# Routing of the first block moved into the last dense turn's up products, and weight splits of the routed layer all on VectorE, in a retention + dense MoE + routed MoE kernel

## The chip, the cores and the metric

One core of one Trainium2 chip runs the whole kernel. The metric is the device time of one execution in microseconds; of several runs the median counts. TensorE (PE in the rows) multiplies, VectorE (DVE) and ScalarE (ACT) do elementwise work, GpSimd (POOL) does elementwise work too and issues indirect DMAs, and SyncE (SP) issues the plain DMAs. Every engine works through its own queue in program order and waits on semaphores of the others.

## The reference, cut to what matters

```
x = attention(q, k, v, lam)                      # N=1536 tokens, model width 512
# dense layer: all E=8 experts on all tokens, F=1024 hidden units, Sinkhorn-like weights P
out = sum_e P[:, e] * (relu(x @ w1[e]) @ w2[e])
# routed layer: every token goes to the one expert with its largest logit
logits = out @ w_gate2
expert_idx = argmax(logits, axis=1)
gate_w = softmax(logits)[arange(N), expert_idx]
final[mask_e] = gate_w * (relu(out[mask_e] @ v1[e]) @ v2[e])
```

Everything is float32. The kernel splits each float32 factor into two float32r parts, `hi` (a rounded copy, made by ScalarE) and `lo` (the rest, made by a subtraction), and takes three products of parts instead of one.

## The kernel before

The dense layer runs in sixteen sub-turns `s` (half an expert's hidden units each), and each of them in two turns `c` of six token tiles. A turn has two calls of `dense_up` (line 536; seven products of six matmuls of 128x384 each, with additions on VectorE between them) and then six tiles of down products (`dense_down`, line 579: twelve matmuls of 128x512 a tile, in two halves of six). `dense_add` (line 588) adds a tile to its sum `acc` on VectorE. `dense_up` calls `between()` at three places; in the last sub-turn that function takes one step from the list `late`.

When `acc` of a tile is complete, `gate2_a` (line 606) writes it to DRAM, transposes it on TensorE (`x2p`, line 611) and copies it by ScalarE; `gate2_b` takes the gate's logits from it (`l2p`, line 618). The routing then runs on VectorE in short instructions: `route_a` (from line 715; the expert of each token and running counts), `route_b` (TensorE, tiles `prank` and `count`), `route_c` (place in the block; `slot` is a 0/1 matrix of token by slot, written for each token tile), `route_first` and `route_first_b` (token numbers of block 0, tile `gid`), and at the end `route_blocks`, `route_slots` (`pid`), `route_experts` and `slot_gates`, `slot_gates_a`, `slot_gates_b` (weights of the slots; an exponential by series, `pgt`).

The routed layer works on blocks of 128 tokens of one expert. For block `b`: an indirect DMA gathers the tokens (`xg`, issued by GpSimd), TensorE transposes them (`xp`), `copy_x` splits them (`xb`), `up` multiplies (`hb`, 24 matmuls in two parts), `turn_h` transposes and splits the hidden units (`hp`, `ht`), `down` multiplies (`yb`, 24 matmuls), and an indirect DMA scatters the result. The weights of an expert are eight pieces of 512 KB; `splitv` (line 654) makes `hi` on ScalarE (line 664) and `lo` by a subtraction of 128x1024 (line 665) on the engine that it is given. `reload` fetches the next expert's pieces into the same room, as soon as the split pieces have been read, and only if the block has another expert.

What sets the order: the schedule is manual, so each engine's queue has the order in which the code issues its instructions. From line 1085 to line 1217 the code is written out by hand: the last six down tiles (called by `dd`), the routing, and the first three blocks, each step in its place. From block 2 on `segment` (line 1214) repeats a fixed order for every block. In the written-out part `splitv` and `split_next` are told which engine subtracts; in `segment` it is VectorE.

Of the kernel before, what the change touches and what calls it, by code (L numbers as in the profile page):

```python
# [10 lines left out]
F32 = mybir.dt.float32  # L11
# [8 lines left out]
P = 128  # L20
# [3 lines left out]
MAGIC = 12583039.0  # 1.5 * 2^23 + 127  # L24
# [7 lines left out]
def tile_retention_moe_moe(  # L32
# [50 lines left out]
    lower = const.tile([P, P], F32, name="lower")  # lower[p, m] = 1 where p < m  # L83
# [17 lines left out]
    # the dense layer takes the tokens in two thirds of CPC tiles of each batch  # L101
# [32 lines left out]
    def load_w2(s):  # L134
        e, o = divmod(s, 2)
        src = w2[e, o * FS:(o + 1) * FS, :].rearrange("(r p) d -> p r d", p=P)
        if s == 0:
            # where the output will be summed
            t = [hpool.tile([P, DM], F32, tag=f"acc{i}", name=f"raw2_0_{i}") for i in (5, 11, 7, 8)]
            for r in range(FS // P):  # L140
                nc.sync.dma_start(out=t[r], in_=src[:, r, :])
            raw[2, s] = t
            return
# [56 lines left out]
    # It leaves the factors of the dense layer: blocks of x^T and their sums, by the halves of  # L200
    # the model width and by the two batches.
# [26 lines left out]
    # decays: dmask[j, h2, pair, i] = lam^(i-j) for i >= j, qpow[(h2 d), pair, i] = lam^(i+1)  # L228
# [32 lines left out]
    def a_transpose(t):  # L261
# [12 lines left out]
        if c < CPB - 1:  # L274
            # from here on, the keys weigh in the state
# [122 lines left out]
    def exp_head(x, tmp):  # L398
        """exp(x) for x <= 0: 2^n by its bits, the rest by its series."""
# [136 lines left out]
    def dense_up(s, c, j, between):  # L536
        """Hidden units j*P.. of either half of FS, for the c-th third of tokens of each batch."""
# [49 lines left out]
    def dense_add(s, t, ps):  # L587
# [3 lines left out]
        if s == 0:  # L591
            # the gate is not ready yet
# [37 lines left out]
    def keep(name, shape, dtype=F32):  # L630
        """One tile for all blocks that take turns in it."""
# [4 lines left out]
    def load_first():  # L636
        # the factors of the dense layer make room, the first blocks before the others
# [16 lines left out]
    def splitv(which, b, j, engine=nc.vector):  # L654
# [14 lines left out]
    # Tiles of tokens in the order of the dense layer's turns; the rank of a token within its  # L669
    # expert is known before the tokens of later turns are.  # L670
# [12 lines left out]
    def route_start():  # L683
        # the blocks' hidden units will take the place of all but the last ones
# [15 lines left out]
        for space, sizes in (  # L700
# [4 lines left out]
            for name, a, b in sizes:  # L705
                r_[name] = space[:, :a * b].bitcast(F32R).rearrange("p (a b) -> p a b", b=b)
                space = space[:, a * b:]

# [568 lines left out]
```

## Time and profile before

| | |
|---|---|
| runs, us | 1337.42, 1331.64, 1329.52 (median 1331.64) |
| the profiled execution's own span | 1330.2 us |
| TensorE busy | 1294.4 us (97%) |
| VectorE busy | 882.5 us (66%) |
| ScalarE busy | 470.8 us (35%) |
| GpSimd busy | 215.2 us (16%) |
| mean granted TensorE clock | 0.986 |

The profile is one execution. In a timeline row stand the start and the duration (us from the span's start), engine, line, operation, output and inputs, their shape, and in brackets how long the engine had been idle and what ended that. PEclk is the granted TensorE clock as a share of 2.4 GHz; it has two levels, 2.4 and 1.2 GHz, so a mean of 0.5 in a stretch means half speed all through it.

### The profile page before, as it was taken

The page shows a single profiled execution, that of the slowest core. Times are in us where ns is not written, and L with a number is a line of the kernel's source. Part 1 is how long each engine was busy: PE and PEld are TensorE (multiplying, and loading weights), DVE is VectorE, ACT ScalarE, POOL GpSimd, SP SyncE. Part 2 cuts the span into 40 slices and gives each one's busy share as a digit, 9 for nine tenths or more (in the row PEclk, how much of TensorE's full clock was granted, in tenths as well). Part 3 has the DMA queues.
Part 4 walks back from the last instruction along what each step waited for, and adds up shares of the span by engine and source line. Part 5 has one row for each costly group of instructions (what it writes and reads, how often), then busy time and mean ns, then how long its engine had stood idle before and what let it go on. Part 6 is the DMA issues. An engine that isn't in the chain of part 4 may idle for free. (4 is left out here: it accounts for less than half of the span.)

```text
span 1330.2 us, 17688 instructions
## 1 busy us (share of the span) xinstructions
PE 1294.4 (97%) x6796; PEld 1144.2 (86%) x6796; DVE 882.5 (66%) x1464; ACT 470.8 (35%) x744; POOL 215.2 (16%) x179
## 2 busy tenths in 40 slices
PE   8999999999999999999999999999999998699998
PEld 6768899999999999999999999999999987578886
DVE  5757756665756656666666575665666466899886
ACT  3433433132222222222313222222222233588885
POOL 5740010101101010101010110101010024631221
PEclk9989999999999999999999999999999988799999
DMA  9610111010101110101001020210000401457463
GB/s 175 152 56 1 32 33 32 33 64 0 64 1 63 32 33 32 32 33 32 32 33 63 1 64 1 64 32 33 32 32 33 174 25 38 153 201 272 158 218 112
DMA packets 73353, 88.79 MB, mean 67 GB/s; under 512 B 41135, under 2 KB 41135, under 8 KB 73264
## 3 DMA queue, kind: packets, MB, share of 16 engines
q1 hardware_dynamic: 70624, 79.74, 19.3%
q0 software_dynamic: 2640, 7.87, 1.8%
q8 instruction: 55, 0.90, 0.3%
q14 instruction: 34, 0.28, 0.1%
HBM read 116.95 MB, written 7.08 MB: 93 GB/s over the span
## 5 line engine op out<-in xcount | busy, mean ns | idle before, releaser
L582 PE MATMUL y<-w2h,h 128*128 128x512 f32 x1536 | 486.6, 393 | 0.0
L529 PE MATMUL p<-xops,w1h 128*128 128x384 f32 x1792 | 455.9, 335 | 0.0
L582 PEld LDWEIGHTS y<-w2h,h 128*128 128x128 f32 x1536 | 290.0, 189 | 59.3
L529 PEld LDWEIGHTS p<-xops,w1h 128*128 128x128 f32 x1792 | 323.9, 188 | 2.4
L582 PE MATMUL y<-w2l,h 128*128 128x512 f32 x768 | 301.0, 392 | 0.0
L529 PE MATMUL p<-xops,w1l 128*128 128x384 f32 x896 | 299.9, 335 | 0.0
L595 DVE SCALAR_TENSOR_TENSOR acc<-y,pm,acc 128x512 f32<-128x512 f32 x180 | 134.9, 750 | 244.1 <-PE y L582 243.5
L545 DVE TENSOR_TENSOR u<-u,p 128x384 f32<-128x384 f32 x320 | 171.0, 551 | 47.6 <-PE p L529 44.0
L549 ACT ACTIVATE h<-u 128x384 fp32r<-128x384 f32 x192 | 101.0, 526 | 282.7 <-DVE u L545 282.7
L557 ACT COPY p<-p 128x384 f32<-128x384 f32 x64 | 30.6, 478 | 396.1 <-PE p L529 396.1
L582 PEld LDWEIGHTS y<-w2l,h 128*128 128x128 f32 x768 | 145.0, 189 | 28.9
L529 PEld LDWEIGHTS p<-xops,w1l 128*128 128x128 f32 x896 | 168.2, 188 | 0.0
L154 POOL TENSOR_TENSOR sums<-raw 128x512 f32<-128x512 f32 x16 | 21.4, 1336 | 814.0 <-DMA raw<-in_moe_w_dram 477.0
L550 DVE SCALAR_TENSOR_TENSOR h<-u,h 128x384 fp32r<-128x384 f32 x192 | 117.0, 609 | 14.2 <-ACT h L549 2.8
L665 DVE TENSOR_TENSOR vl<-room,vh 128x1024 fp32r<-128x1024 f32 x82 | 101.2, 1281 | 13.6 <-ACT vh L664 13.0
L664 ACT CAST vh<-room 128x1024 fp32r<-128x1024 f32 x88 | 88.2, 1061 | 10.5 <-DMA room<-in_moe_w_dram 10.5
L1064 PE MATMUL yb<-vh,ht 128*128 128x512 f32 x224 | 72.8, 396 | 0.0
L545 DVE TENSOR_TENSOR u<-p,p 128x384 f32<-128x384 f32 x64 | 35.3, 552 | 54.5 <-PE p L529 54.4
L1064 PE MATMUL yb<-vl,ht 128*128 128x512 f32 x112 | 44.6, 398 | 8.6 <-DVE vl L665 8.6
L1064 PEld LDWEIGHTS yb<-vh,ht 128*128 128x128 f32 x224 | 42.6, 191 | 9.7 <-DVE ht L1054 0.7
L1032 PE MATMUL hb<-room,xb 128*128 128x512 f32 x168 | 41.0, 394 | 0.0
L182 DVE TENSOR_TENSOR w2l<-raw,w2h 128x512 fp32r<-128x512 f32 x64 | 40.0, 686 | 1.2 <-ACT w2h L181 1.2
(220 smaller groups left out, 1227.2 us busy)
## 6 DMA issues: line engine op xcount, KB each, us to landing
room<-in_moe_w_dram SPq DMA_DIRECT2D x132, 512.0 KB
raw<-in_moe_w_dram SPq DMA_DIRECT2D x31, 1024.0 KB
q<-in_q_dram SPq DMA_DIRECT2D x12, 256.0 KB
k<-in_k_dram SPq DMA_DIRECT2D x12, 256.0 KB
v<-in_v_dram SPq DMA_DIRECT2D x12, 256.0 KB
x2d<-acc SPq DMA_DIRECT2D x12, 256.0 KB
raw<-in_moe_w_dram SPq DMA_DIRECT2D x4, 256.0 KB
xg<-x2d,gid POOLq DMA_INDIRECT x16, 4.6
```

Source lines behind the costliest of these rows:

```text
L182: nc.vector.tensor_tensor(out=lo, in0=raw[2, s][r], in1=f32(hi), op=ALU.subtract)
L529: nc.tensor.matmul(ps, lhsT=w[:, a, k, j * P:(j + 1) * P], rhs=xops[c][:, b, part, k, :], start=(n == 0), stop=(n == 5),)
L545: nc.vector.tensor_tensor(out=out, in0=in0, in1=in1, op=ALU.add)
L549: nc.scalar.activation(hi, x, AF.Relu)
L550: nc.vector.scalar_tensor_tensor(out=lo, in0=x, scalar=0.0, in1=f32(hi), op0=ALU.max, op1=ALU.subtract)
L557: nc.scalar.copy(p1, mul(A11, B11))
L582: nc.tensor.matmul(ps, lhsT=h[f][:, part, o * P:(o + 1) * P], rhs=w[:, f, :], start=(j == 0 and f == j and i == 0), stop=(j == 1 and f != ...
L595: nc.vector.scalar_tensor_tensor(out=acc[t], in0=ps, scalar=pm[:, t, e:e + 1], in1=acc[t], op0=ALU.mult, op1=ALU.add,)
L664: nc.scalar.copy(hi, t)
L665: engine.tensor_tensor(out=lo, in0=t, in1=f32(hi), op=ALU.subtract)
L1032: nc.tensor.matmul(ps, lhsT=x[:, kk, :], rhs=w[:, cols], start=(n == 0), stop=(n == 3 * KD - 1))
L1064: nc.tensor.matmul(ps, lhsT=h[:, f, :], rhs=w[:, f % 2, :], start=(n == 0), stop=(n == 3 * KF - 1),)
```

## The change

1. `splitv` and `split_next` have no engine to choose any more: every `lo` of the routed layer's weights is subtracted by VectorE. The six `slot` matrices of the first turn, too, are written by VectorE and no longer by GpSimd (`route_c` loses its engine).
2. The routing of the first block (`route_ones`, `route_a`, `route_b`, `route_c`, `route_first`, `route_first_b`, `gather(0)`) becomes four entries at the end of `late`, and so runs during the two `dense_up` calls of the last turn. It writes its six slot matrices to a place of its own (`early["slot"]`, in the former weights' room), since the final place still holds factors of the dense layer; they are written a second time, to the final place, after the second split.
3. The steps of the written-out part are reordered: transposes and logits of finished tiles come two tiles later or closer together, `route_slots` comes before `route_experts`, `up(1, 0)` comes ahead of the splits of block 1's second weights, and `slot_gates` with `slot_gates_a` moves from before and between those splits to after block 1's `turn_h`. The subtraction that `slot_gates` began with moves into `route_experts`.

```
-    def splitv(which, b, j, engine=nc.vector):
+    def splitv(which, b, j):
...
         nc.scalar.copy(hi, t)
-        engine.tensor_tensor(out=lo, in0=t, in1=f32(hi), op=ALU.subtract)
+        nc.vector.tensor_tensor(out=lo, in0=t, in1=f32(hi), op=ALU.subtract)
...
+        early["slot"] = words("raw", [P, KD, FS], F32R, "early_slot").rearrange(
+            "p (a b) -> p a b", b=P)
...
-    def route_c(p0, p1, engine=vt):
+    def route_c(p0, p1):
...
+        if p0 > 0:
+            slots(p0, p1, r_["slot"])
+
+    def slots(p0, p1, dst):
         for p in range(p0, p1):
-            engine.tensor_scalar(
-                out=r_["slot"][:, p], in0=ioff, scalar1=off[:, p - p0:p - p0 + 1], scalar2=None,
+            vt.tensor_scalar(
+                out=dst[:, p], in0=ioff, scalar1=r_["off"][:, p:p + 1], scalar2=None,
                 op0=ALU.is_equal,
             )
...
                     if o == 2 * CPC - 1:
                         late.append(gate2)
+                        late.append(lambda: (route_ones(), route_a(0, 2 * CPC)))
+                        late.append(lambda: route_b(0, 2 * CPC))
+                        late.append(lambda: (
+                            route_c(0, 2 * CPC), slots(0, 2 * CPC, early["slot"]), route_first()))
+                        late.append(lambda: (route_first_b(), gather(0)))
...
-    def split_next(which, b, j0, j1, engines=(nc.vector,)):
+    def split_next(which, b, j0, j1):
...
     ps = {}
-    route_ones()
-    route_a(0, n0)
-    splitv(1, 0, 0, nc.gpsimd)
-    splitv(1, 0, 1, nc.gpsimd)
+    g_a, g_b = (lambda i: gate2_a(turns[n0 + i])), (lambda i: gate2_b(turns[n0 + i]))
     dd(0, 0)
     dd(1, 0)
     dd(0, 1)
+    splitv(1, 0, 0)
     dd(1, 1)
+    splitv(1, 0, 1)
+    slots(0, n0, r_["slot"])
+    dd(2, 0)
+    g_a(0)
     splitv(1, 0, 2)
-    gate2_a(turns[n0])
-    route_b(0, n0)
-    route_c(0, n0, nc.gpsimd)
-    route_first()
-    dd(2, 0)
...
     run(ups)
     route_blocks()
     turn_h(0, (0,))
+    splitv(2, 0, 3)
+    route_slots()
     route_experts()
     reload(1, 1)
     reload(2, 1)
-    route_slots()
     turn_h(0, (1,))
     gather(1)
-    slot_gates()
     downs = down(0)
-    run(downs, 3 * KF - 4)
+    run(downs, 3 * KF - 6)
     turn_x(1, copies=False)
-    run(downs, 4)
+    run(downs, 6)
...
-    split_next(1, 1, 0, KD - 1, (v_, p_, v_))
+    split_next(1, 1, 0, KD - 1)
     copy_x(1)
     split_next(1, 1, KD - 1, KD)
-    slot_gates_a()
-    split_next(2, 1, 0, KD, (v_, p_, p_, p_))  # E1
     run(up(1, 0))
+    split_next(2, 1, 0, KD)
     run(up(1, 1))
     turn_h(1, (0,))
     turn_x(2)
     gather(4)
     turn_h(1, (1,))
-    split_next(1, 2, 0, KD, (v_, p_))  # E2
+    slot_gates()
+    slot_gates_a()
+    split_next(1, 2, 0, KD)
     downs1 = down(1)
     run(downs1, 2 * KF)
     slot_gates_b()
     run(downs1, KF)
-    split_next(2, 2, 0, KD, (v_, p_))  # E3
+    split_next(2, 2, 0, KD)
```

TensorE's queue in the last turn's second `dense_up`: `p_15_1_1` are its products (the number at the end tells them apart), first before, then of the change.

```order
L529 MATMUL p_15_1_1_8736<-xops_100,w1h_8253 128x384 x2
L529 MATMUL p_15_1_1_8736<-xops_100,w1l_8254 128x384
L529 MATMUL p_15_1_1_8744<-xops_100,w1h_8253 128x384 x2
L529 MATMUL p_15_1_1_8744<-xops_100,w1l_8254 128x384
L529 MATMUL p_15_1_1_8744<-xops_100,w1h_8253 128x384 x2
```

```order
L529 MATMUL p_15_1_1_8751<-xops_100,w1h_8253 128x384 x2
L529 MATMUL p_15_1_1_8751<-xops_100,w1l_8254 128x384
L750 MATMUL prank_8759<-early_x 128x48
L751 MATMUL prank_8759<-early_x 128x48
L529 MATMUL p_15_1_1_8762<-xops_100,w1h_8253 128x384 x2
```

The two `prank` products stand between the second and the third of the seven products now; the one `full` product comes after the fourth, and the six `pid` products after the seventh.

VectorE's queue from block 1's input split to the second weights of block 2: `vl` are weight parts, `xb` and `ht` the parts of inputs and hidden units, L874 to L885 before (L885 to L902 now) the slot gates. Before:

```order
L1019 TENSOR_TENSOR xb_1_9239<-xp_9193,xb_1_9238 128x512
L665 TENSOR_TENSOR vl_3_1_9243<-room_8478,vh_3_1_9242 128x1024
L874 TENSOR_TENSOR room_8479<-room_8478,tok_88 128x12x20
L416 SCALAR_TENSOR_TENSOR room_8478<-room_8478 128x96 x6
...
L884 CAST room_8479<-room_8478 128x12x20
L885 TENSOR_TENSOR room_8479<-room_8478,room_8479 128x12x20
L665 TENSOR_TENSOR vl_0_1_9284<-room_8478,vh_0_1_9283 128x1024
L1054 TENSOR_TENSOR ht_9216<-hp_0_9327,ht_9215 128x512
L1019 TENSOR_TENSOR xb_0_9340<-xp_9334,xb_0_9339 128x512
L1054 TENSOR_TENSOR ht_9216<-hp_1_9344,ht_9215 128x512
L665 TENSOR_TENSOR room_8479<-room_8478,room_8479 128x1024 x2
```

and now:

```order
L1035 TENSOR_TENSOR xb_1_9240<-xp_9192,xb_1_9239 128x512
L665 TENSOR_TENSOR vl_3_1_9244<-room_8478,vh_3_1_9243 128x1024
L665 TENSOR_TENSOR vl_0_1_9284<-room_8478,vh_0_1_9283 128x1024
L665 TENSOR_TENSOR vl_1_1_9288<-room_8478,vh_1_1_9287 128x1024
L665 TENSOR_TENSOR vl_2_1_9220<-room_8478,vh_2_1_9219 128x1024
L665 TENSOR_TENSOR vl_3_1_9222<-room_8478,vh_3_1_9221 128x1024
L1070 TENSOR_TENSOR ht_9217<-hp_0_9313,ht_9216 128x512
L1035 TENSOR_TENSOR xb_0_9326<-xp_9320,xb_0_9325 128x512
L1070 TENSOR_TENSOR ht_9217<-hp_1_9330,ht_9216 128x512
L885 TENSOR_SCALAR lg<-lg 128x96
...
L902 TENSOR_TENSOR room_8479<-room_8478,room_8479 128x12x20
L665 TENSOR_TENSOR room_8479<-room_8478,room_8479 128x1024 x4
```

The gates moved behind the hidden units of block 1, and VectorE has all four subtractions of each set.

GpSimd's queue from the start of the routed layer's work to the first scatter (`L1002` and `L819` are gathers). Before:

```order
L665 TENSOR_TENSOR room_8479<-room_8478,room_8479 128x1024 x2
L766 TENSOR_SCALAR room_8479<-ioff,room_8478 128x128 x6
L1002 DMA early_x<-x2d,gid 128x512
L665 TENSOR_TENSOR room_8479<-room_8478,room_8479 128x1024
L665 TENSOR_TENSOR early_l<-room_8478,early_h 128x1024 x3
L665 TENSOR_TENSOR early_r<-room_8478,early_r 128x1024
...
L665 TENSOR_TENSOR vl_1_1_9231<-room_8478,vh_1_1_9230 128x1024
L665 TENSOR_TENSOR vl_1_1_9288<-room_8478,vh_1_1_9287 128x1024
```

and now:

```order
L716 TENSOR_SCALAR early_x<-ones 128x8
L819 DMA early_x<-x2d,gid 128x512 x2
L819 DMA xg_9223<-x2d,gid 128x512
L819 DMA xg_9225<-x2d,gid 128x512
L819 DMA xg_9223<-x2d,gid 128x512
L1088 DMA out_dram<-room_8478,sid 1536x512
```

Fifteen subtractions and six slot matrices have left it; gathers and scatters remain.

## Rows read from the trace of the kernel before

**Rows 1.** Windows: busy time of PE, PEld, DVE, ACT, POOL; PEclk, DMA share, GB/s

```profile
1172.20:1320.00 147.80, 147.80 (x730) 123.94 (x729) 133.84 (x135) 129.07 (x169) 30.53 (x25) 1.00 0.60 211
```

**Rows 2.** Timeline of TensorE: its longest waits before 1172 us

```profile
1087.27 0.66 PE L611 MATMUL x2p<-ident,acc 128*128 128x128 f32 x4 [3.19 <-DVE acc L595]
1135.91 1.04 PE L1032 MATMUL hb<-vh,xb 128*128 128x512 f32 x2 [1.88 <-DVE xb L1019]
1153.08 0.79 PE L1064 MATMUL yb<-vl,ht 128*128 128x512 f32 x1 [8.59 <-DVE vl L665]
```

**Rows 3.** Windows as in rows 1: the stretch after the first of these waits

```profile
1088.00:1094.70 6.70, 6.70 (x23) 5.49 (x23) 2.73 (x11) 0.59 (x1) 3.50 (x6) 0.53 0.21 78
```

**Rows 4.** Timeline of VectorE: long instructions of the routing, slot gates and splits

```profile
1081.20 2.06 DVE L726 TENSOR_TENSOR early_x<-room,ioff 128x48 fp32r<-128x48 f32 x1
1083.37 3.18 DVE L730 TENSOR_TENSOR early_x<-early_x 128x8 fp32r<-128x8 f32 x6
1139.41 6.01 DVE L416 SCALAR_TENSOR_TENSOR room<-room 128x96 f32<-128x96 f32 x6
1147.07 2.36 DVE L884 CAST room<-room 128x240 fp32r<-128x240 f32 x1
1160.41 5.77 DVE L665 TENSOR_TENSOR vl<-room,vh 128x1024 fp32r<-128x1024 f32 x2
```

**Rows 5.** Single lines on VectorE: ns min/median/max, first and last start

```profile
L724 DVE TENSOR_TENSOR early_x<-early_x,ioff x3: 207/2264/2305, 1080.7 to 1117.6; 128x24 fp32r<-128x24 f32 x2, 128x48 fp32r<-128x48 f32 x1
L416 DVE SCALAR_TENSOR_TENSOR etmp<-etmp x6: 258/258/259, 114.8 to 116.3; 128x96 f32<-128x96 f32 x6
L874 DVE TENSOR_TENSOR room<-room,tok x1: 2574/2574/2574, 1136.9 to 1136.9; 128x240 fp32r<-128x240 f32 x1
L885 DVE TENSOR_TENSOR room<-room,room x1: 2426/2426/2426, 1149.5 to 1149.5; 128x240 fp32r<-128x240 f32 x1
L665 DVE TENSOR_TENSOR room<-room,room x27: 1209/1218/1221, 1087.8 to 1303.5; 128x1024 fp32r<-128x1024 f32 x27
```

**Rows 6.** Timeline of VectorE: the same kinds while GpSimd did nothing

```profile
1107.25 0.57 DVE L730 TENSOR_TENSOR early_x<-early_x 128x8 fp32r<-128x8 f32 x3
1124.87 0.41 DVE L834 TENSOR_TENSOR room<-room,row 128x240 fp32r<-128x240 f32 x1
```

**Rows 7.** Timeline of GpSimd: its first two subtractions

```profile
1080.77 4.75 POOL L665 TENSOR_TENSOR room<-room,room 128x1024 fp32r<-128x1024 f32 x2 [60.46 <-ACT room L664]
```

**Rows 8.** Timeline: end of VectorE's first `dense_up`; TensorE's last product, down products, third tile

```profile
1071.82 1.23 DVE L550 SCALAR_TENSOR_TENSOR h<-u,h 128x384 fp32r<-128x384 f32 x2
...
1077.39 0.51 PE L529 MATMUL p<-xops,w1h 128*128 128x384 f32 x2
1078.43 0.39 PE L582 MATMUL y<-w2h,h 128*128 128x512 f32 x1
1083.69 0.39 PE L582 MATMUL y<-w2h,h 128*128 128x512 f32 x1
1088.02 0.48 PE L582 MATMUL y<-w2h,h 128*128 128x512 f32 x1
```

**Rows 9.** Timeline of TensorE: one tile's distance; of VectorE: from `count` to `val`

```profile
1098.24 0.48 PE L582 MATMUL y<-w2h,h 128*128 128x512 f32 x1
1102.34 0.49 PE L582 MATMUL y<-w2h,h 128*128 128x512 f32 x1
1121.10 0.26 DVE L813 TENSOR_TENSOR room<-count,i 128x96 f32<-128x96 f32 x1 [0.36 <-PE count L743]
```

**Rows 10.** Timeline: `pid`, expert list, block 1's casts, its first activation, two kinds of splits

```profile
1125.33 1.77 PE L843 MATMUL pid<-room 128*128 128x20 f32 x12
1127.53 0.16 DVE L860 TENSOR_TENSOR other<-room 1x19 int32<-1x19 f32 x1
1129.50 2.95 ACT L664 CAST vh<-room 128x1024 fp32r<-128x1024 f32 x3 [1.26 <-DMA room<-in_moe_w_dram]
1140.14 0.60 ACT L1037 ACTIVATE room<-hb 128x512 f32<-128x512 f32 x1 [2.18 <-POOL vl L665]
1152.94 0.68 DVE L1054 TENSOR_TENSOR ht<-hp,ht 128x512 fp32r<-128x512 f32 x1
1169.22 4.63 DVE L665 TENSOR_TENSOR vl<-room,vh 128x1024 fp32r<-128x1024 f32 x4 [0.16 <-ACT vh L664]
```

More of the change, by code (lines that the diff above doesn't have):

```diff
@@ L707, in route_start @@
                 space = space[:, a * b:]
+        early["slot"] = words("raw", [P, KD, FS], F32R, "early_slot").rearrange(
+            "p (a b) -> p a b", b=P)
+        early["xg"] = [early["x"][:, b * DM:(b + 1) * DM] for b in range(2)]
     def route_ones():
@@ L800, in route_first_b @@
             nc.tensor.matmul(
-                pid[:, :2], lhsT=r_["slot"][:, p], rhs=r_["val0"][:, p],
+                pid[:, :2], lhsT=early["slot"][:, p], rhs=r_["val0"][:, p],
                 start=(p == 0), stop=(p == 2 * CPC - 1),
@@ L805, in route_first_b, with gather @@
             out=gid[:, 0:1], in0=pid[:, 0:1], scalar1=-1.0, scalar2=0.0, op0=ALU.add, op1=ALU.max
+        )
+    xg = {}
+    def gather(b):
+        xg[b] = early["xg"][b] if b < 2 else keep(f"xg{b % 2}", [P, DM])
+        nc.gpsimd.indirect_dma_start(
+            out=xg[b], out_offset=None, in_=x2d[:2 * CPC * P, :] if b == 0 else x2d,
+            in_offset=bass.IndirectOffsetOnAxis(ap=gid[:, b:b + 1], axis=0),
         )
@@ L861, in route_experts @@
         vt.tensor_copy(nal, end[0:1, E - 1:E])
-    def slot_gates():
         vt.tensor_tensor(
@@ L867, in slot_gates @@
         )
+    def slot_gates():
         vt.tensor_scalar_max(lgf, lgf, -87.0)
@@ L981, in tile_retention_moe_moe @@
     ereg = {}
-    xg, xt, xb, hb, ht = {}, {}, {}, {}, {}
+    xt, xb, hb, ht = {}, {}, {}, {}
     def reload(which, b):
@@ L998, in reload @@
             nc.sync.dma_start(out=rawv[which, j], in_=src, cond=new)
-    def gather(b):
-        xg[b] = early["xg"][b] if b < 2 else keep(f"xg{b % 2}", [P, DM])
-        nc.gpsimd.indirect_dma_start(
-            out=xg[b], out_offset=None, in_=x2d[:2 * CPC * P, :] if b == 0 else x2d,
-            in_offset=bass.IndirectOffsetOnAxis(ap=gid[:, b:b + 1], axis=0),
-        )
     def turn_x(b, copies=True):
@@ L1080, in run @@
             pass
-    def split_next(which, b, j0, j1, engines=(nc.vector,)):
+    def split_next(which, b, j0, j1):
         if b < NB:
             for j in range(j0, j1):
-                splitv(which, b, j, engines[j % len(engines)])
+                splitv(which, b, j)
             if j1 == KD and b + 1 < NB:
@@ L1098, in tile_retention_moe_moe @@
     )
-    early["xg"] = [early["x"][:, b * DM:(b + 1) * DM] for b in range(2)]
     def dd(o, j):
@@ L1115, in tile_retention_moe_moe @@
     dd(0, 1)
+    splitv(1, 0, 0)
     dd(1, 1)
+    splitv(1, 0, 1)
+    slots(0, n0, r_["slot"])
+    dd(2, 0)
+    g_a(0)
     splitv(1, 0, 2)
-    gate2_a(turns[n0])
-    route_b(0, n0)
-    route_c(0, n0, nc.gpsimd)
-    route_first()
-    dd(2, 0)
-    gate2_b(turns[n0])
     dd(2, 1)
-    gate2_a(turns[n0 + 1])
+    g_b(0)
     dd(3, 0)
-    route_first_b()
-    gather(0)
-    splitv(1, 0, 3, nc.gpsimd)
-    gate2_b(turns[n0 + 1])
+    g_a(1)
+    splitv(1, 0, 3)
     dd(3, 1)
-    gate2_a(turns[n0 + 2])
-    splitv(2, 0, 0, nc.gpsimd)
-    splitv(2, 0, 1, nc.gpsimd)
+    g_b(1)
+    turn_x(0)
     dd(4, 0)
-    gate2_b(turns[n0 + 2])
+    g_a(2)
+    splitv(2, 0, 0)
+    dd(4, 1)
+    g_b(2)
     route_a(n0, n1)
-    dd(4, 1)
-    gate2_a(turns[n1])
-    turn_x(0)
+    g_a(3)
     dd(5, 0)
-    gate2_b(turns[n1])
+    g_b(3)
+    g_a(4)
+    splitv(2, 0, 1)
     route_b(n0, n1)
-    gate2_a(turns[n1 + 1])
     dd(5, 1)
+    g_b(4)
+    route_c(n0, n1)
     early["ht"] = tuple(
@@ L1149, in tile_retention_moe_moe @@
     )
-    gate2_b(turns[n1 + 1])
-    gate2_a(turns[n1 + 2])
-    splitv(2, 0, 2, nc.gpsimd)
-    splitv(2, 0, 3, nc.gpsimd)
-    route_c(n0, n1)
-    ups = itertools.chain(up(0, 0), up(0, 1))
-    run(ups, 5)
-    gate2_b(turns[n1 + 2])
+    ups = itertools.chain(up(0, 0), up(0, 1))
+    run(ups, 2)
+    g_a(5)
+    splitv(2, 0, 2)
+    run(ups, 4)
+    g_b(5)
     route_a(n1, NT)
-    run(ups, 10)
+    run(ups, 9)
     route_b(n1, NT)
@@ L1187, in tile_retention_moe_moe @@
             keep(f"v{part}2_{j}_1", [P, 2, DM], F32R)
-    v_, p_ = nc.vector, nc.gpsimd
     gather(2)
     gather(3)
-    split_next(1, 1, 0, KD - 1, (v_, p_, v_))
+    split_next(1, 1, 0, KD - 1)
     copy_x(1)
     split_next(1, 1, KD - 1, KD)
-    slot_gates_a()
-    split_next(2, 1, 0, KD, (v_, p_, p_, p_))
     run(up(1, 0))
+    split_next(2, 1, 0, KD)
     run(up(1, 1))
```

## The prediction

> **What bounds the kernel now.** First read the windows. From 1172.2 us on TensorE is busy without a gap at full clock for 147.8 us [rows 1], and the change leaves the order of that part alone: it shortens the kernel by as much as it brings the point forward at which block 3's first up product (`hb` of part 0) ends, 1172.2 us. Ahead of it, read TensorE's timeline for waits. The longest all end in a VectorE instruction: 3.19 us for the sum of a tile, 1.88 us for block 1's input, 8.59 us for its weight part [rows 2]. Each costs more than itself: in the stretch after the first, the granted clock was 0.53, that is the lower of its two levels, 1.2 GHz, nearly throughout [rows 3].
>
> Then see why VectorE is late. An addition of a 128x8 set took 0.19 us in one place (three in 0.57) and six took 3.18 in another; a 128x48 mask took 2.06, six exponential steps 6.01, a 128x240 cast 2.36 [rows 4]. The same lines or shapes ran in 0.207 and 0.258 [rows 5], or 0.41 [rows 6], where GpSimd had nothing to do. The long ones lie beside GpSimd's subtractions, the first of which ran from 1080.77 for 4.75 us [rows 7]. The excess that these rows show: L724 twice, 4.15; L726 1.85; L730 2.04; L416 4.46; L874 2.16; L884 1.95; L885 2.02; the two splits at 1160.41, 3.34. Together 22.0 us [rows 4 to 6].
>
> **The change part by part.** *Subtractions to VectorE.* GpSimd needs about 2.4 us for one (4.75 for two [rows 7]), VectorE 1.21 [rows 5]. Fifteen move: 18.2 us more on VectorE. Six slot matrices move and six are written twice: twelve instructions of 128x128, at the 0.26 of a 128x96 one [rows 5], 3.1 us. So VectorE takes over 21.3 us and loses at least 22.0 of excess: its work is about even. The gain must come from the order, from waits that go, and from 5.7 us of routing (2.4 and 3.3, below) that now lie under the up products.
>
> Here the Trainium skill speaks on both sides. "Perfetto Trace Analysis", section "Optimizing Scalar/DVE Operations", says that with a saturated VectorE moving work to GpSimd may make sense, but adds that the two share an SBUF read port, so that it might not help. By its first half alone the change would cost 18.2 us of VectorE time. "SBUF — State Buffer", section "Who interferes with whom", says that a VectorE instruction with two SBUF inputs and a GpSimd instruction that reads SBUF exclude one another for a whole instruction; by that all 22.0 us go. This trace agrees with the second: 0.207 against 2.3 us for one line.
>
> I follow the new order through four points on TensorE's queue.
>
> *Point A, start of the third tile's down products, 1088.0 before* [rows 8]. A product of the up phase takes 1.04 us, and the last ended at 1078.43, so the second one of that `dense_up` ended at 1073.2. Now `prank` comes next and waits for `route_a`. VectorE is free of the first `dense_up` at 1073.05 [rows 8]; five short instructions at 0.24 make the masks by 1074.3, six additions at 0.19 [rows 6] end at 1075.4, so TensorE is 2.2 us late at 1075.5. Queued behind it are five products (5.2 us). Does the clock fall? A wait of 1.88 us was followed by half rate at once [rows 2]: ten `hb` matmuls took it from 1135.91 to about 1140.0, where their activation follows [rows 10]. I take half rate for 4.5 us, which costs 2.25: the products end at 1083.0. The first two of them end at 1079.7; VectorE has its additions for these by 1080.8, then `route_c` (five at 0.24), six slots and four instructions of `route_first` (0.2 each): 1084.0 to 1084.1. `pid` (0.6) waits for these; then 24 down matmuls, 5.5 us [rows 8]: **1090.2**, 2.2 us later than before. Before, the same place had the 3.19 us wait; VectorE's unfinished additions no longer bring it about, since each tile's transpose now stands a tile or more behind its sum.
>
> *Point B, start of the `pid` products that number all slots, 1125.3 before* (0.41 us after 1124.87 [rows 9]). One tile with its transposes and logits takes 4.1 us at full rate [rows 9]. Four make 16.4; two more sets of transposes and logits 2.4; block 0's transpose and `prank` 0.6; 14 `hb` matmuls 3.2; I add 1.2 for two waits on masks that VectorE still has in hand. `count` starts at 1114.0 and ends at 1114.4; from there to `val` VectorE needs 4.2 us (1121.1 to 1125.3 [rows 9]), and the ten other `hb` matmuls lie under that: **1118.6**, 6.7 us earlier. TensorE waits some 1.5 us here.
>
> *Point C, end of block 1's first `hb` part, about 1140.0 before.* `pid` takes 1.7 us (1.77 [rows 10]), `gid` and the expert list 1.3; the list's last entry to ScalarE's first cast took 1.97 us (1127.53 to 1129.50 [rows 10]). First cast at 1123.3, first subtraction at 1124.3; three at 1.17 and the input's 0.68 [rows 10]: 1128.5. Ten matmuls: 2.3 us at full, 4.3 at half rate: **1131 to 1133**, 7 to 9 us earlier.
>
> *Point D, end of block 3's first `hb` part, 1172.2 before.* Now all is VectorE's chain. Activation 0.7 and cast 1.0, then four subtractions 4.8: 6.5. Three 128x512 splits 1.9 [rows 10]. The slot gates without excess 6.2: six head steps 1.6, the series 1.55 [rows 5], the three of 240 columns 1.3 [rows 6], six small ones 1.7. Then four subtractions 4.7, `gate` 0.6, four more 4.7, a split 0.65, block 3's four 4.7 (4.63 [rows 10]), and three matmuls 0.7. Sum 30.7: **1161.6 to 1163.7**. Before, the same chain had the gates ahead of block 1's second weights, and TensorE's 8.59 us wait was for them; its next wait, for `pgt`, is about 4 us now, but under VectorE's chain and so free.
>
> GpSimd's remaining gathers are hidden: `gather(0)` is issued some 8 us ahead of its transpose. SyncE's queue keeps its order; block 2's second weights are fetched about 15 us earlier than before, since their room is read earlier, so ScalarE's waits for them should go.
>
> D moves by 8.5 to 10.6; I take **9.6**. The span 1330.2 becomes 1320.6; the median of the runs is 1.4 above that span, so the forecast is **1322.0 us**, 0.7% faster.
>
> Open prices. The clock: with no fall at A and C the gain is 10.6 + 2.2 = 12.8; with a fall as long as the 6.7 us stretch [rows 3], 1.1 less than 8.5: 7.4. The 240-column gate instructions alone never ran undisturbed: nearest row 0.41 [rows 6], upper end their 2.4 [rows 5]; the upper end takes up to 6 us away (gain 3.6), and I take the lower, the shape being the same.
>
> **The rivals.** *The clock stays up.* The new waits at A, B and C are 1 to 2 us each, all shorter than the 3.19 us one; against it stands the 1.88 us row. Gain 12.8, with splits at 1.16 rather than 1.21 up to 14: 1318 to 1319.
>
> *The wait only moves.* TensorE goes slow at A and, with a second wait for `pid` there, stays slow until its queue runs dry, as it did from 1088 to 1094.7 [rows 3]: 7 us more at half rate, half of it regained where VectorE bounds, and each next step late by it. Gain 2 to 4: about 1329. For it speaks that A is the one place that gets worse.
>
> *VectorE becomes the bound (slower).* If its long instructions are long for another reason than GpSimd, the 22.0 us stay while 21.3 us come on top: 9.6 − 22.0, 1344. It decides against the change from 44% of the excess (9.6 of 22.0) on. For it speaks that VectorE's chain, by the working above, sets the pace up to D; against it that one line ran in 0.207 us just ahead of GpSimd's first subtraction and ten times that beside it. This is the case that the skill's advice to move work away from a saturated VectorE would lead to.
>
> **How the numbers follow.** Forecast 0.55 (own range 1317 to 1326), clock stays up 0.22, wait only moves 0.15, VectorE the bound 0.08. The range reaches over the first three: 1313 to 1332. About 1% is what a measurement of this kernel can tell from no change, and 13.3 us is 1%. The fast rival passes it in most of its cases and the forecast's tail in a few: faster 0.27; slower only the last, 0.08; the rest, 0.65, within 1%.
>
> **What would show it.** Right: L724, L416 and the gates at 0.2 to 0.4 us; TensorE waiting about 2 us for `prank` near 1073, low clock after; the third tile starting near 1090; `val` near 1118; the 8.59 us wait gone and one of 4 us for `pgt` in its place; block 3's first part ending near 1163, and the rest 158 us as before. Wrong: long instructions on VectorE without GpSimd beside them, a TensorE wait for a gather, or ScalarE waiting for weights in blocks 2 and 3.

## The result and the profile after

Five runs of the changed kernel took 1317.83 to 1321.96 us, median 1319.88; five of the kernel before, beside them, 1329.52 to 1337.42, median 1331.89. The ratio is 0.9908 (95% interval 0.9882 to 0.9935): 12.0 us faster, 0.9%, "within 1%" by a little. The forecast was 1322.0.

The profiled executions were 1330.2 and 1316.1 us long, 14.1 apart. The one of the changed kernel was the fastest of its five runs: 1317.83 us at a mean granted clock of 0.996, where the four others took 1319.52 to 1321.96 at 0.990 to 0.992. Not all of the 14.1 is the change, either. One activation of the dense stage, 870 us ahead of anything that was moved, is already 1.46 us earlier after than before; the two rows are from ScalarE's timeline, of before and of after:

```profile
202.24 0.53 ACT L549 ACTIVATE h<-u 128x384 fp32r<-128x384 f32 x1 [3.70 <-DVE u L545]
```

```profile
200.78 0.53 ACT L549 ACTIVATE h<-u 128x384 fp32r<-128x384 f32 x1 [3.70 <-DVE u L545]
```

All comparisons below are therefore made from this **start mark**. Two more marks follow the change: **P**, the start of the twelve `pid` products that number all slots (point B of the prediction), and **D'**, the start of the last product with a lower weight part in block 3's first part, 0.6 us ahead of point D (before: 1171.63). TensorE's timeline after shows P, D', the last product of that part, and the waits on the way (in brackets: idle time, and what ended it):

```profile
1072.82 0.26 PE L750 MATMUL prank<-early_x 128*128 128x48 f32 x1 [0.88 <-DVE early_x L729]
...
1073.89 0.26 PE L751 MATMUL prank<-early_x 128*128 128x48 f32 x1 [0.81 <-DVE early_x L733]
...
1080.40 0.83 PE L807 MATMUL pid<-early_x,early_slot 128*128 128x2 f32 x6 [0.81 <-DVE early_x L799]
...
1115.87 1.85 PE L859 MATMUL pid<-room 128*128 128x20 f32 x12 [1.29 <-DVE room L850]
...
1142.39 1.50 PE L907 MATMUL pgt<-room 128*128 128x60 f32 x12 [3.57 <-DVE room L902]
...
1157.31 0.49 PE L1048 MATMUL hb<-vl,xb 128*128 128x512 f32 x1 [0.17 <-DVE vl L665]
...
1157.65 0.39 PE L1048 MATMUL hb<-vh,xb 128*128 128x512 f32 x1
```

The 3.19 us wait for a tile's sum and the 8.59 us wait for a weight part [rows 2] are gone. In their place stand two of 0.88 and 0.81 for the masks of block 0, 0.81 for its slots, 1.29 ahead of `pid` and 3.57 ahead of `pgt`. One long wait is missing from [rows 2], although it is longer than the 1.88 us there: 2.87 us for the masks that `count` sums. It is 0.36 now (before, then after):

```profile
1120.49 0.58 PE L743 MATMUL count<-early_x 128*128 128x8 f32 x4 [2.87 <-DVE early_x L726]
```

```profile
1110.90 0.61 PE L746 MATMUL count<-early_x 128*128 128x8 f32 x4 [0.36 <-DVE early_x L729]
```

VectorE's timeline after shows why TensorE waits less:

```profile
1072.46 0.21 DVE L729 TENSOR_TENSOR early_x<-room,ioff 128x48 fp32r<-128x48 f32 x1
1072.78 1.17 DVE L733 TENSOR_TENSOR early_x<-early_x 128x8 fp32r<-128x8 f32 x6
...
1121.69 3.50 DVE L665 TENSOR_TENSOR vl<-room,vh 128x1024 fp32r<-128x1024 f32 x3 [1.67 <-issue]
...
1130.03 4.66 DVE L665 TENSOR_TENSOR vl<-room,vh 128x1024 fp32r<-128x1024 f32 x4 [3.10 <-ACT vh L664]
...
1138.15 1.72 DVE L416 SCALAR_TENSOR_TENSOR room<-room 128x96 f32<-128x96 f32 x6
...
1141.84 0.41 DVE L902 TENSOR_TENSOR room<-room,room 128x240 fp32r<-128x240 f32 x1
```

The 128x48 mask (L729, L726 before) runs in 0.21 us where it took 2.06, the six additions behind it in 1.17 (3.18), the six exponential steps in 1.72 (6.01), the 128x240 subtraction in 0.41 (2.43) [rows 4, 5]. GpSimd issues only gathers and scatters in this stretch. Two gaps of VectorE, 1.67 us up to 1121.69 and 3.10 up to 1130.03, will matter below. Two windows of after (columns as in [rows 1]):

```profile
1076.00:1083.00 7.00, 6.19 (x35) 5.54 (x35) 6.37 (x23) 1.87 (x4) 0.00 (x0) 1.00 0.00 1
1158.00:1305.00 147.00, 147.00 (x726) 123.03 (x725) 133.21 (x135) 129.04 (x169) 28.58 (x24) 1.00 0.58 209
```

The clock stayed at full speed after the new waits (PEclk 1.00 from 1076 to 1083), and from point D on TensorE is busy without a gap as in [rows 1].

### The profile page after: what moved, and what is told of

Same layout as the page of the kernel before. It is cut to its first block, busy times and chain, and to the rows that moved or that the text cites. A ratio compares the mean times of both kernels' runs of the same rounds, so it can differ in the third digit from the quotient of the medians.

```text
span 1316.1 us, 17691 instructions
## 1 busy us (share of the span) xinstructions
PE 1286.6 (98%) x6796; PEld 1138.5 (87%) x6796; DVE 873.5 (66%) x1491; ACT 470.1 (36%) x744; POOL 172.8 (13%) x158
## 4 chain that ended last, share of the span: by engine, by line
PE 81%; issue 10%; DMA 4%; DVE 2%; POOL 2%; ACT 1%; POOLq 0%; SPq 0%; DVEq 0%; ACTq 0%
PE y L582 40%; PE p L529 35%; DMA out_dram<-room,sid 2%; DMA out_dram<-y,sid 2%; PE o L314 1%; PE s L292 1%; PE o L310 1%; POOL xr L330 1%; POOL xg L819 1%; PE l2p L618 1%; PE kv L346 1%; DVE xops L337 1%; PE x2p L611 0%; PE pq L267 0%; PE pk L267 0%
## 5 line engine op out<-in xcount | busy, mean ns | idle before, releaser
L665 DVE TENSOR_TENSOR vl<-room,vh 128x1024 fp32r<-128x1024 f32 x88 | 103.0, 1220 | 18.0 <-ACT vh L664 15.6
```

The source lines that it names most:

```text
L665: nc.vector.tensor_tensor(out=lo, in0=t, in1=f32(hi), op=ALU.subtract)
```

## The experiments

All marks in one table, each from the timeline of one profiled execution. "Gain" is how much less D' lies behind the start mark than before (969.39 us); beside it the gain of the median time against runs of the kernel before on the same chip. Two kernels have a single run.

| kernel | start mark | P | D' | start to P | P to D' | gain of D' | gain of the time |
|---|---|---|---|---|---|---|---|
| before | 202.24 | 1125.33 | 1171.63 | 923.09 | 46.30 | | |
| after | 200.78 | 1115.87 | 1157.31 | 915.09 | 41.44 | 12.9 | 12.0 |
| old order, VectorE (e1) | 200.88 | 1116.45 | 1154.68 | 915.57 | 38.23 | 15.6 | 14.0 |
| new order, GpSimd (e2) | 202.46 | 1117.51 | 1175.58 | 915.05 | 58.07 | -3.7 | -2.5 |
| routing behind (e3) | 201.87 | 1113.95 | 1156.26 | 912.08 | 42.31 | 15.0 | 15.7 |
| gates ahead (e4) | 202.20 | 1118.80 | 1157.50 | 916.60 | 38.70 | 14.1 | 13.7 |
| old order, late part (e5) | 202.49 | 1124.29 | 1163.46 | 921.80 | 39.17 | 8.4 | 7.8 |
| dead subtractions (e6) | 202.45 | 1119.03 | 1166.85 | 916.58 | 47.82 | 5.0 | 4.4 |
| dead memsets (e7) | 202.35 | 1118.63 | 1160.83 | 916.28 | 42.20 | 10.9 | 10.1 |
| both orders undone (b1) | 202.24 | 1114.27 | 1152.72 | 912.03 | 38.45 | 18.9 | 18.1 |

The last two columns agree within 1.6 us in every row: the time goes where D goes, as the prediction had it. A difference of 1 to 2 us between two rows can still be that of two executions of one program; e1's profile, like that of the kernel after, is of its fastest run (1315.24 us, the three others 1317.88 to 1318.4).

**e1: the engine without the order.** The kernel before, with only this:

```
-        engine.tensor_tensor(out=lo, in0=t, in1=f32(hi), op=ALU.subtract)
+        nc.vector.tensor_tensor(out=lo, in0=t, in1=f32(hi), op=ALU.subtract)
...
-            engine.tensor_scalar(
+            vt.tensor_scalar(
```

> The kernel before in its old order, with one part of the change alone: all fifteen subtractions and the six slot matrices of the first turn go from GpSimd to VectorE. Theory (what GpSimd does beside VectorE makes VectorE's instructions long, and the order is needed besides): L724, L730, L416, L884 to L888 run in 0.2 to 0.4 us as in the kernel after, VectorE's 22.0 us of excess go and 18.2 us of subtractions come, and the time falls by 1 to 7 us (ratio to the kernel before 0.995 to 0.999), about half of the 12.0 us of the whole change or less. Rival 1 (the order does nothing, the engine is all): ratio 0.991 as the whole change. Rival 2 (VectorE becomes the bound; long instructions for another reason than GpSimd): L416 stays near 1 us each, ratio above 1.005.

Measured: 1317.9 us, ratio 0.9892 (0.9853 to 0.9931). The theory named the right mechanism but asked for an order as well; that half fell. The choice of the engine alone gives as much as the whole change; whether it gives more, the overlapping intervals don't tell. TensorE's timeline (P, D' and its two longest waits), then VectorE's:

```profile
1111.51 0.58 PE L743 MATMUL count<-early_x 128*128 128x8 f32 x4 [2.89 <-DVE early_x L726]
...
1116.45 1.71 PE L843 MATMUL pid<-room 128*128 128x20 f32 x12
...
1136.49 0.73 PE L1064 MATMUL yb<-vh,ht 128*128 128x512 f32 x2 [3.44 <-DVE ht L1054]
...
1154.68 0.50 PE L1032 MATMUL hb<-vl,xb 128*128 128x512 f32 x1 [0.16 <-DVE vl L665]
```

```profile
1127.18 1.72 DVE L416 SCALAR_TENSOR_TENSOR room<-room 128x96 f32<-128x96 f32 x6
...
1131.20 4.63 DVE L665 TENSOR_TENSOR vl<-room,vh 128x1024 fp32r<-128x1024 f32 x4
```

The gates stand where they stood, ahead of block 1's second weights, and the exponential steps take 1.72 us for 6.01. The waits of 3.19, 1.88 and 8.59 us [rows 2] have become 1.60, 0.80 and, now for the hidden units, 3.44; the one for `count` stays. VectorE does fifteen subtractions and six slot matrices more and is yet busy for 870.7 us over the whole span, where it was 882.5. Of these 11.8 us, 3.2 lie in the dense stage, which is the same in both; from there to D' the difference is 8.5 (73.46 us for 81.99). By stretches, from the first down product to P and from P to D', before and then e1 (columns as in [rows 1]):

```profile
1078.43:1125.33 46.90, 39.90 (x194) 33.12 (x193) 31.15 (x79) 13.57 (x19) 21.29 (x14) 0.86 0.11 40
1125.33:1171.63 46.30, 34.95 (x155) 27.10 (x154) 40.86 (x52) 28.27 (x35) 27.94 (x15) 0.85 0.35 118
```

```profile
1077.07:1116.45 39.38, 34.83 (x194) 29.18 (x194) 29.08 (x92) 13.57 (x19) 1.91 (x1) 0.96 0.13 47
1116.45:1154.68 38.23, 33.04 (x155) 25.88 (x155) 34.39 (x60) 28.08 (x35) 7.32 (x7) 0.95 0.47 156
```

VectorE is busy for 66% of the first stretch before and for 74% in e1, and for 88% and 90% of the second.

**e2: the order without the engine.** The kernel after, with the fifteen subtractions given back (the slot matrices stay on VectorE):

```
-    splitv(1, 0, 0)
+    splitv(1, 0, 0, nc.gpsimd)
...
-    split_next(1, 2, 0, KD)
+    split_next(1, 2, 0, KD, (v_, p_))
```

> The kernel after in its new order, with the same fifteen subtractions given back to GpSimd (the slot matrices stay on VectorE). Theory: GpSimd's subtractions take 2.4 us each, VectorE's instructions beside them are long again (the slot gates, 5.85 us in the kernel after, over 10 us), and of the 12.0 us at least 7 are lost: ratio to the kernel before 0.996 to 1.004. Rival 1 (the order is all): ratio 0.991, as the kernel after. Rival 2 (GpSimd's help outweighs its disturbance, 18.2 us less on VectorE): below 0.989.

Measured: 1334.37 us, ratio 1.0012 (0.9994 to 1.0029): nothing is left of the gain. The two stretches tell it apart. Up to P the new order helps by itself: 915.05 us, as in the kernel after, 8.0 less than before. There e1 gains 7.5 by the engine alone and the kernel after 8.0 by both, so either will do and the two do not add up. From P to D' e2 is 16.6 us worse than after. The three timelines, of GpSimd, VectorE and TensorE:

```profile
1144.82 4.65 POOL L665 TENSOR_TENSOR room<-room,room 128x1024 fp32r<-128x1024 f32 x2
1149.42 4.63 POOL L665 TENSOR_TENSOR vl<-room,vh 128x1024 fp32r<-128x1024 f32 x2
```

```profile
1144.10 0.26 DVE L405 SCALAR_TENSOR_TENSOR room<-room,lg 128x96 f32<-128x96 f32 x1
1144.39 9.78 DVE L408 SCALAR_TENSOR_TENSOR room<-room 128x96 f32<-128x96 f32 x1
1154.21 0.21 DVE L411 TENSOR_SCALAR room<-room 128x96 f32<-128x96 f32 x1
```

```profile
1117.51 1.48 PE L859 MATMUL pid<-room 128*128 128x20 f32 x12 [1.28 <-DVE room L850]
...
1158.89 2.74 PE L907 MATMUL pgt<-room 128*128 128x60 f32 x12 [15.35 <-DVE room L902]
...
1175.58 0.51 PE L1048 MATMUL hb<-vl,xb 128*128 128x512 f32 x1 [0.17 <-DVE vl L665]
```

One step of 128x96 (L408) that takes 0.26 us elsewhere lasted 9.78: it began 0.43 us ahead of GpSimd's four subtractions in a row (1144.82) and ended 0.12 us behind them (1154.05). The new order had put the gates right beside them, and TensorE's wait for `pgt` grew from 3.57 to 15.35 us.

**e6 and e7: the disturbance by itself.** The kernel after, with work on GpSimd that nobody needs, beside the gates; VectorE's own work is the same. e6:

```
+    idle = room[0][:, 8 * F + 512:9 * F]
+    h0, h1 = (f32(ht[1][i][:, KF // 2:]).rearrange("p a b -> p (a b)") for i in range(2))
+    nc.gpsimd.tensor_copy(idle[:, :1], h1[:, :1])
+    for _ in range(4):
+        nc.gpsimd.tensor_tensor(out=idle, in0=h0, in1=h1, op=ALU.subtract)
     slot_gates()
```

In e7 the loop runs ten times over `nc.gpsimd.memset(idle, 0.0)`. `h0` and `h1` are the two parts of the second half of block 1's transposed hidden units, `idle` is room that nothing else uses then.

> The kernel after with four more subtractions of 128x512 on GpSimd, whose result nobody reads, one behind another beside VectorE's slot gates (first one as soon as the second lower part of block 1's transposed hidden units is written). VectorE does the same work as in the kernel after. Theory (VectorE's instructions wait for GpSimd's that read SBUF): each takes 1.2 to 1.5 us, at least one of the gates' instructions lasts as long as one of them or the whole row, and the gates take 9 to 11 us in place of 5.85; the time is 2 to 5 us longer. Rival (the long instructions have another reason, such as the shape or the place of the operands): the gates stay at 5.85 us and the time is that of the kernel after.

> The same with ten memsets of 128x512 on GpSimd, which read nothing, in place of the four subtractions (0.53 us each in the attention stage of the trace of before). If it is GpSimd's reading of SBUF with two operands that holds VectorE up: the gates stay at 5.85 us, within 0.3. If any work of GpSimd on SBUF does: 9 to 11 us as with the subtractions.

Measured: 1327.09 and 1321.46 us (one run each). With the subtractions, GpSimd's and VectorE's timelines:

```profile
1139.90 5.34 POOL L1215 TENSOR_TENSOR room<-ht,ht 128x512 f32<-128x512 f32 x4
```

```profile
1139.71 0.21 DVE L401 TENSOR_SCALAR room<-lg 128x96 f32<-128x96 f32 x1
1139.96 1.30 DVE L404 TENSOR_SCALAR room<-room 128x96 f32<-128x96 f32 x1
1141.30 1.37 DVE L405 SCALAR_TENSOR_TENSOR room<-room,lg 128x96 f32<-128x96 f32 x1
1142.70 1.31 DVE L408 SCALAR_TENSOR_TENSOR room<-room 128x96 f32<-128x96 f32 x1
1144.05 1.26 DVE L411 TENSOR_SCALAR room<-room 128x96 f32<-128x96 f32 x1
1145.23 0.40 DVE L891 TENSOR_TENSOR room<-room,tok 128x240 fp32r<-128x240 f32 x1
```

Four instructions in turn take 1.26 to 1.37 us where they take 0.2 to 0.3, each about as long as one of GpSimd's subtractions (5.34 / 4 = 1.34), and the lines are quick again as soon as GpSimd is done. L885 to L902 take 10.15 us for 5.85, 4.3 more, and so does TensorE's wait for `pgt` (7.89 us for 3.57). P to D' grows by 6.4; what makes the 2 us that the wait does not explain is not shown. The one time is 7.2 us above the median of the kernel after, more than the 2 to 5 that were expected; 1.5 us come ahead of P, where nothing was changed (see e4). With the memsets:

```profile
1139.27 5.83 POOL L1215 MEMSET room<- 128x512 f32 x10
```

```profile
1139.36 0.50 DVE L404 TENSOR_SCALAR room<-room 128x96 f32<-128x96 f32 x1
...
1139.89 0.26 DVE L405 SCALAR_TENSOR_TENSOR room<-room,lg 128x96 f32<-128x96 f32 x1
...
1140.48 0.54 DVE L411 TENSOR_SCALAR room<-room 128x96 f32<-128x96 f32 x1
...
1143.52 0.45 DVE L896 TENSOR_SCALAR rs<-rs 128x12 f32<-128x12 f32 x1
...
1144.71 0.54 DVE L901 CAST room<-room 128x240 fp32r<-128x240 f32 x1
```

Here a tensor_scalar of one input (L404, L411, L896) or the cast (L901) takes 0.45 to 0.54, about one memset (0.58), and steps with two inputs (L405) keep their 0.26; one tensor_scalar in the row, L419 with an int32 result, keeps its 0.20. The gates take 6.80 us, 0.95 more, outside the 0.3 that was allowed: what GpSimd reads is most of it, not all. The Trainium skill ("SBUF — State Buffer", section "Who interferes with whom") has both halves: a VectorE instruction with two SBUF inputs excludes a GpSimd one that reads SBUF but not one that only writes, while cast and tensor_scalar can enter a mode in which they contend with either. These rows agree, by 1.37 against 0.26 us for L405 and 0.54 against 0.21 for L411. The prediction had the first half alone, which does not cover L884, a cast of one input with 1.95 of its 22.0 us.

**e5: one part of the engine change.** The kernel before, with the eight later subtractions alone on VectorE:

```
-    split_next(2, 1, 0, KD, (v_, p_, p_, p_))
+    split_next(2, 1, 0, KD)
```

(and the same for the three other calls with a list of engines).

> The kernel before in its old order, with only the eight later subtractions (blocks 1 and 2: one, three, two and two) moved to VectorE; the seven of block 0 and the six slot matrices stay on GpSimd. In the run with all of them moved (old order, VectorE alone) the start of the numbers of all slots came 7.5 us earlier against the same point of the dense stage, and the stretch from there to the end of block 3's first up product shrank from 46.9 to 38.75 us, 8.1 less. Theory (each move pays where GpSimd's operation stood beside VectorE's, and the two parts add up): 8 us faster than before, ratio 0.993 to 0.995, the gates L874 to L885 in 4.6 us again, the long additions near 1081 to 1086 and 1102 to 1120 unchanged. Rival 1 (the gain needs the first block's part, since only what comes early is handed on): ratio 0.998 or more. Rival 2 (all is in the late part, the early shift is swallowed by a wait): 0.990 or less.

Measured: 1323.71 us, ratio 0.9949 (0.9929 to 0.9969). P and D' on TensorE:

```profile
1124.29 1.85 PE L843 MATMUL pid<-room 128*128 128x20 f32 x12 [1.17 <-DVE room L834]
...
1163.46 0.50 PE L1032 MATMUL hb<-vl,xb 128*128 128x512 f32 x1 [0.18 <-DVE vl L665]
```

P to D' is 39.17 us, 7.1 less than before; start to P gains only 1.3. Of e1's 7.5 and 8.1 us for the two stretches, 6.2 and 0.9 are left for the seven earlier subtractions and the six slot matrices, by difference; no run has these alone.

**e3 and e4: two parts of the order undone.** e3 takes block 0's routing out from under the up products and puts it about where it stood; block 0's transpose (`turn_x(0)`) comes one tile later with it:

```
-                        late.append(lambda: (route_ones(), route_a(0, 2 * CPC)))
-                        late.append(lambda: route_b(0, 2 * CPC))
...
+    route_ones()
+    route_a(0, n0)
     dd(0, 0)
     dd(1, 0)
     dd(0, 1)
     splitv(1, 0, 0)
     dd(1, 1)
+    route_b(0, n0)
+    route_c(0, n0)
...
```

> The kernel after with the routing of block 0 back behind the up products (masks and sums ahead of the first down products, ranks and slots after the first two tiles, the numbers of block 0 after the fourth tile's first half, its transpose after the fifth tile). The prediction's step (5.7 us of VectorE's routing gain by lying under the up products): 3 to 6 us slower than the kernel after, ratio to the kernel before 0.993 to 0.996. Rival, from the trace of after: TensorE's waits of 0.88, 0.81 and 0.81 us for these masks go, and VectorE, which is idle for 1.60, 2.14, 1.93 and 1.63 us in the down products, takes the 5.7 us in there: as fast as the kernel after or up to 2.5 us faster, ratio 0.989 to 0.991.

Measured: 1316.24 us (1315.81 to 1316.94), ratio 0.9878 (0.9839 to 0.9917). The expected loss did not come; the kernel is faster than the one after, whose five runs all lie above 1317.8. P and D':

```profile
1113.95 1.48 PE L859 MATMUL pid<-room 128*128 128x20 f32 x12 [1.28 <-DVE room L850]
...
1156.26 0.50 PE L1043 MATMUL hb<-vl,xb 128*128 128x512 f32 x1 [0.17 <-DVE vl L665]
```

Start to P shrinks by 3.0 us: the 2.5 us of waits for masks and slots are gone, and VectorE found room for the routing between the tiles' sums. P to D' is 0.9 longer, so that D' gains 2.1 over the kernel after; the medians differ by 3.6.

e4 puts the slot gates back:

```
     gather(1)
+    slot_gates()
...
     split_next(1, 1, KD - 1, KD)
+    slot_gates_a()
...
-    slot_gates()
-    slot_gates_a()
     split_next(1, 2, 0, KD)
```

> The kernel after with the slot gates back where they stood: their first part after the gather of block 1, the second ahead of the split of block 1's second weights. The prediction's step (the 6.2 us wait behind the block's second weights so that TensorE gets these sooner): 2 to 6 us slower than the kernel after, ratio to the kernel before 0.993 to 0.996, with a TensorE wait for block 1's second weights of 3 us or more. Rival, from the trace of after: VectorE is idle for 1.67 us up to 1121.69 and 3.10 us up to 1130.03 there, since ScalarE's casts come after the activation of block 1's first part; the gates fill these gaps, the subtractions are 1.3 us later, and the 5.85 us at 1136.40 go: 3 to 4.5 us faster than the kernel after, ratio 0.987 to 0.989.

Measured: 1318.23 us, ratio 0.9888 (0.9846 to 0.9929); by the times alone not to be told from the kernel after, and not the loss of 2 to 6 us that the prediction's step asked for. The trace tells more. TensorE's P and D', and a window:

```profile
1118.80 1.49 PE L859 MATMUL pid<-room 128*128 128x20 f32 x12 [1.28 <-DVE room L850]
...
1157.50 0.50 PE L1048 MATMUL hb<-vl,xb 128*128 128x512 f32 x1 [0.16 <-DVE vl L665]
```

```profile
1076.00:1083.00 7.00, 6.55 (x30) 6.23 (x28) 4.00 (x17) 0.53 (x1) 0.00 (x0) 0.77 0.01 4
```

P to D' is 38.70 us, 2.7 less than after: the gates now fill the two gaps of VectorE that were named above, and TensorE's longest wait there is 2.04 us, for the hidden units and not for a weight part. But start to P is 1.5 longer, though nothing there was changed: behind the same waits of 0.88 and 0.81 us the clock fell in this execution (PEclk 0.77 from 1076 to 1083), which it had not in the kernel after (1.00).

**b1: both undone.** The edits of e3 and e4 together:

> The kernel after with both orders undone that were seen not to pay: block 0's routing behind the up products again, and the slot gates where they stood; all subtractions stay on VectorE. Against the same point of the dense stage, block 0's routing behind the up products brought the numbers of all slots 1.9 us earlier (1113.95 less 1.10 of an earlier difference between the executions, against 1115.87 less 0), and the gates ahead shortened the stretch from there to the end of block 3's first up product from 42.0 to 39.2 us. If both add up: 4.7 us faster than the kernel after, 1315 us, ratio 0.986 to 0.988. If VectorE, which then bounds the whole stretch, takes the one back: as the better of the two alone, 1316 to 1318, ratio 0.988 to 0.990.

Measured: 1313.39 us (1313.23 to 1313.6), ratio 0.9868 (0.9852 to 0.9885): faster than both kernels, 18.1 us below the one before and 6.5 below the one after (6.1, if each is taken against its own runs of before). P and D':

```profile
1114.27 1.48 PE L859 MATMUL pid<-room 128*128 128x20 f32 x12 [1.29 <-DVE room L850]
...
1152.72 0.50 PE L1043 MATMUL hb<-vl,xb 128*128 128x512 f32 x1 [0.17 <-DVE vl L665]
```

Both stretches keep their gain (912.03 and 38.45 us), so the two add up, and more than the 4.7 us that were expected, since the 1.9 us for the early stretch were the bare difference of the two rows (1115.87 less 1113.95), without the shift of the start mark that makes them 3.0.

## Why the prediction was right, and where it was not

**The time.** 1319.88 lies within the range and within the likeliest case's own 1317 to 1326, 2.1 us under the forecast. The profile can't say where these 2.1 came from, since its execution is the fastest of the five and 4.5 us under the forecast span of 1320.6: 1.46 by the start mark, the rest by D. The points below are those of this execution; the column "shifted" adds the 1.46 us to after's row, so that it can be read against the forecast:

| point | forecast | after | shifted | difference |
|---|---|---|---|---|
| A, third tile | 1090.2 | 1086.6 (24 products from 1081.09) | 1088.1 | -2.1 |
| B, `pid` | 1118.6 | 1115.87 | 1117.3 | -1.3 |
| C, end of block 1's first part | 1131 to 1133 | 1128.46 (its activation) | 1129.9 | -2.1 from the middle |
| D | 1161.6 to 1163.7 | 1158.0 (1157.65 + 0.39) | 1159.5 | -3.1 from the middle |

*A.* The wait came as forecast: 0.88 + 0.81 and the matmul between, 2.1 us. The mis-sized term is the half rate behind it, for which 2.25 us were taken from the 1.88 us row [rows 2]: in the profiled execution the clock did not fall. It is a matter of the execution, not of the kernel. after, e2, e4, e6 and e7 have the same instructions up to there. In after and e2 the granted clock from 1076 to 1083 was 1.00, in e4, e6 and e7 it was 0.77, 0.78 and 0.76. The last three share after's program up to P, too, and their start to P is 916.28 to 916.60 us against 915.09: in these executions the fall costs 1.2 to 1.5 us, not 2.25. At A, the forecast and the rival "the clock stays up" were two outcomes of one program, with a smaller price between them than thought. The profiled execution followed the rival; whether the clock fell there in the four slower runs is not known. At C the ten products ran at full rate as well.

*B to D.* `count` to `val` took 4.2 us and the expert list to the first cast 1.97, both as forecast; the gates took 5.85 for 6.2 and four subtractions 4.63 to 4.66 for 4.7 to 4.8; the chain from C to D was 29.6 us for 30.7. The wait for `pgt` was 3.57 for 4, and free as forecast. So the forecast time was no mere luck: its chains took VectorE's instructions at their undisturbed length, and so they ran.

**The reason.** Here the prediction failed, in one step: "So VectorE takes over 21.3 us and loses at least 22.0 of excess: its work is about even. The gain must come from the order, from waits that go, and from 5.7 us of routing". e1, without the order, gains 14.0 us, and e2, with the order and the slot matrices but without the subtractions, gains nothing over the whole. Waits did go, but e1 shortens those of [rows 2] by the engine alone; only the 2.87 us for `count` needed the order (2.89 in e1, 1.19 in e2, 0.36 with both). And point B's 6.7 us by the order are borne out by e2, which gains 8.0 up to P, only that the engine gives nearly the same there without the order.

Two things were wrong in the sum. One is its size. The 22.0 us were a floor and were used as the value: up to D', VectorE's busy time in e1 is 8.5 us less with 18.2 of subtractions and 1.3 of slot matrices more to do, so about 28.0 went (an estimate from the windows and rows of before and e1). Left out were, in the trace of before, L721 twice, 1.51 and 1.73 us for 0.18, and a subtraction of 2.78 for 1.21. The other is that one sum was made for two unlike stretches. Up to P, VectorE idled for a third of the time before, and what counts there is what stands ahead of the instruction that TensorE waits for: ahead of the tile's sum, 3.9 us of excess went (L726 and L730 [rows 4]) and two subtractions of 2.35 came, so the wait of 3.19 us is 1.6 shorter. That has a sequel on TensorE, as the prediction had said of waits: of the 7.5 us by which P is nearer in e1, 2.5 are idle time, and 5.1 are that the same 194 matmuls keep it busy for 34.83 us and not 39.90, at a mean granted clock of 0.96 for 0.86. From P to D', VectorE is nearly full, 88% before and 90% in e1, and there its work itself shrank: 9.7 us came, about 16.2 went, 6.5 less, and the stretch is 8.1 shorter.

The parts of the order, each read from one execution: the routing under the up products costs 3.0 us up to P (e3; the prediction counted 5.7 us as a gain, though it saw the 2.2 us wait); the gates behind block 1's second weights cost 2.7 from P to D' (e4; the prediction credited them with the end of the 8.59 us wait, which the engine alone had cut to 3.44, and overlooked that VectorE is idle just there). Both together make the 6.0 us of D', and 6.1 of the time, by which b1 leads the kernel after. What is left of the order gains 3.3 (D' of b1 against e1; 4.1 by the times), all of it ahead of P: e1 waits there 1.60 us for the third tile's sum and 2.89 for `count`, b1 not at all and 0.36. Which of the moves ends these waits no run has alone; the prediction's remark that each tile's transpose now stands a tile or more behind its sum names a likely one. That the whole order costs anything against the old order on VectorE (2.7 us by D', 2.0 by the times) is not shown, since the intervals of e1 and of the kernel after overlap.

**The rivals.** "The wait only moves" did not come about: the new waits did not keep TensorE slow until D. "VectorE becomes the bound" had its condition wrong by e6, in which GpSimd's work alone, with VectorE's unchanged, brings the long instructions back. "The clock stays up" is what the profiled execution shows at A and C.

## What to carry to other kernels

Where a VectorE instruction is long only beside a GpSimd one, price the move stretch by stretch and not by one sum. Where VectorE has idle time, look at what stands ahead of the instruction that TensorE waits for: here 3.9 us of excess went from there and 2.35 of new work came. Where VectorE is nearly full, weigh all the excess that goes, every long instruction and not a choice of them, against the work that comes: here 16.2 us against 9.7. A change that moves an engine and an order should be taken apart before either is credited; here the engine alone gave as much as the whole, the order alone nothing over the whole, and two of its moves ate a third of what was to be had. Marks ahead of the change and around it compare two single profiles to better than 2 us where their spans do not.

## What the runs showed of the hardware that was not expected

- A VectorE instruction can be held for a whole row of GpSimd instructions, not only for one: L408, 9.78 us across four subtractions that began after it (e2), while in e6 each of four VectorE instructions was held for just one. Why it got its turn in between in one case and not in the other stays open; no run tells it apart.
- The same two waits of TensorE, 0.88 and 0.81 us, were followed by full clock in two executions and by a granted clock of 0.76 to 0.78 from 1076 to 1083 us in three.
- GpSimd's memsets, which read nothing, lengthened a one-input VectorE step from 0.21 to 0.54 us (L411), and left a two-input one at 0.26 (L405) and a one-input one with an int32 result at 0.20 (L419).
